# Attention output in four 64x64 quarters, with the state read where it is computed, and a new order of the steps

## Chip, cores and metric

The kernel runs on one core of one Trainium2 chip. The metric is the device time of one run in microseconds. 635.68 us is the median of three runs of the kernel before (635.10 to 636.07).

## What is computed

Three parts follow each other: a linear attention with a decaying state, a mixing layer with sine and cosine, and a gated feed-forward layer. The reference, cut:

```python
# q, k, v, alpha: (4, 8, 768, 48)
for t in range(S):
    state = alpha[:, :, t, :, None] * state + np.einsum('bhd,bhe->bhde', k[:, :, t], v[:, :, t])
    y[:, :, t] = np.einsum('bhd,bhde->bhe', q[:, :, t], state)
...
x = np.ascontiguousarray(attn_out.transpose(0, 2, 1, 3)).reshape(B, S, H * D)   # (4, 768, 384)
theta = x @ w_theta
zr, zi = x * np.cos(theta), x * np.sin(theta)
u = x + np.einsum('ts,bsd->btd', w_tok_r, zr) + np.einsum('ts,bsd->btd', w_tok_i, zi)
x = u + np.maximum(u @ w_ch, 0.0)
...
h = np.maximum(x @ w_in, 0.0)
u, v = h[..., :512], h[..., 512:]
v_n = (v - mean(v)) / sqrt(var(v) + 1e-06)
v_s = np.einsum('ts,bsd->btd', w_spatial, v_n) + b_spatial[None, :, None]
out = (u * v_s) @ w_out
```

## The kernel before

**Units.** The attention is cut into 24 units, `u = 6*b + i`: batch `b` (4) and block `i` of 128 times (6). A unit holds 8 heads, as four pairs `a` of two heads (`par` 0 and 1), and the 128 times as two chunks `c` of 64. On the partitions the heads of a pair stand at 0 to 47 and 64 to 111, or the chunk times of both heads at 0 to 63 and 64 to 127.

**Steps of a unit.** `load_al`, `load_qk`, `load_vn`, `load_vt` are DMAs on SP's queue. VectorE scans the decays (`att_scan`, two scans and a reciprocal) and makes decayed keys and queries (`att_kh`, `att_qh`). TensorE multiplies them: A (`att_a`) gives the 64x64 products of times, which VectorE masks into the tile `am` (`att_mask`, one instruction for each half `e` of the pairs, pairs with `a % 2 == e`); K (`att_k`) transposes the keys, which ScalarE copies out (`att_kt`); U (`att_u`) gives each chunk's addition to the state. VectorE carries the state on from chunk to chunk (`att_s` decays it into the tile `ss`, `att_t` adds U's result). Y (`att_y`) is the output: masked product times values, plus queries times state. ScalarE copies it out of PSUM as `x` (`att_x`). Then TensorE transposes `x` (P, `tr_p`), VectorE splits it into a high and a low part (`tr_l`), TensorE multiplies with `w_theta` (theta, `th_p`, in two halves of 6 and 3 matmuls), ScalarE and VectorE make the sines (`th_k` to `z_m`), the result is split again (`z_h` on ScalarE, `z_l` on VectorE), and TensorE mixes times (T, `tokmix`, six steps of 6 matmuls per unit into the accumulators `acc`). After the six units of a batch come `evac` and the channel layer (`ch_h` to `ch_d`). The last part (`v_p`, `g_u`, `g_s`, `o_p` and what belongs to them) begins near 375 us and isn't touched.

**How Y works before.** Y multiplies both heads of a pair at once, with 96 columns: 112 or 128 partitions go in, and 64 come out for each chunk, so that two chunks stand side by side in the 128x64 form. For this the state and the values must stand block-diagonally: the tiles `sd` and `vd` hold one head's rows against its own 48 columns and zeros elsewhere. `fill` sets the zeros once, on GpSimd; `load_vt` writes the values in two DMAs per unit; `move_s` moves the state out of `ss` in two DMAs per chunk. The output of all heads stands in one PSUM bank. A and U use four 64x64 quarters of the array.

**PSUM.** Five banks are the accumulators of T. Three buffers `ps` are shared by A (two at a time), U (two), K, Y, P, theta and the channel products (one each).

**Weights.** The weights come as float64, are turned into float32 and split by VectorE and ScalarE (`bits`, `join`, `mul`, `low`, `sgn`, `sign`, `mag`, `high`), 30 pieces of them during the first batch. Their DMAs (`raw`) stand on GpSimd's queue.

**Order.** Nothing in a loop sets the order. Each step is entered in a table with its engine, its cost, its buffers and what it waits for. `latest` counts back from due times, to which offsets by the step's name (`OFF`, `OFF0` for the first batch, `OFF3` for the last), unit (`UNIT`) and weight piece (`PIECE`) are added. `order` plays the table through and takes on each free engine the ready step with the earliest time whose buffers are free. The steps are then written out in that order, and each engine works through its own list strictly in it. SP's queue is such a list too.

Of the kernel before, what the change touches and what calls it, by code (L numbers as in the profile page):

```python
# [49 lines left out]
    "bits": 29.93, "sgn": -32.28, "mag": -28.48, "mul": -75.34, "high": -103.47, "low": 39.61, "v": 4.81, "vr": 68.54,  # L50
    "vb": 201.01, "vw": 0.03, "vm": -10.46, "vh": -39.63, "vl": -128.02, "g_u": 6.32, "g_r": -35.97, "g_s": -34.57,
    "g_m": -185.78, "g_h": -102.29, "g_l": 52.98, "o_p": -1.97, "o_e": 72.74, "x2h": 240.17, "x2l": 9.57,
    "x2": -58.05,
# [15 lines left out]
}  # L69
OFF3 = {  # L70
# [21 lines left out]
SSB = 2  # L92
PE_WINDOW = 4096 / 1200
PE_BUSY = {"att_a": 0.78, "att_u": 0.85, "att_y": 0.7}


def order(steps):
# [21 lines left out]
    free = dict.fromkeys(ready, 0.0)  # L119
    port = 0.0  # L120
# [14 lines left out]
    while heap:  # L135
# [11 lines left out]
        while moved:  # L147
            moved = False
            for e, q in ready.items():
# [3 lines left out]
                while q:  # L153
                    _, k = heapq.heappop(q)
# [75 lines left out]
def attention_mixer_kernel(  # L230
# [50 lines left out]
    sdt = []  # L281
    vdt = []
# [871 lines left out]
```

## Time and profile before

| | |
|---|---|
| median of three runs | 635.68 us |
| span of the profiled execution, first to last instruction | 630.0 us |
| median run less span | 5.68 us |
| TensorE matmuls busy | 589.7 us, 94% of the span |
| VectorE busy | 438.3 us, 70% |
| ScalarE busy | 285.1 us, 45% |
| GpSimd busy | 33.0 us, 5% |
| mean DMA rate | 98 GB/s |

The profile is of one execution, of which the page gives the span alone; its whole time is taken as the median, 5.68 us above the span. "Busy" is the union of an engine's instruction times; matmuls overlap in the array, so the time a step costs TensorE is read as the distance from its first matmul to the first one of the next step. Each float32 matmul of the program leaves two records in the trace, so Y's 16 matmuls per part are 32 records together. A row of the timeline gives start, time, engine, source line, operation, written tile and read tiles, and in brackets the idle time ahead of it with what ended it.

### The profile page before, as it was taken

What the parts mean: (1) busy time and instruction counts of PE and PEld (TensorE: products, weight loads), DVE (VectorE), ACT (ScalarE), POOL (GpSimd) and SP (SyncE); (2) the same over time, 40 slices, a digit from 0 to 9 for tenths busy, and PEclk for the clock granted to TensorE, in tenths of its full rate; (3) what the DMA queues carried; (4) which work ended last, traced back from release to release, by engine and by line L of the source; (5) the groups of instructions that cost most, each with busy time, mean ns of one, the idle gap of its engine ahead of it and who ended that gap; (6) DMA issues with size and microseconds to landing.
All of it is one profiled execution on the core that took longest, in us unless ns stands there. A gap on an engine that the chain in (4) does not pass through costs nothing.

```text
span 630.0 us, 13096 instructions
## 1 busy us (share of the span) xinstructions
PE 589.7 (94%) x5364; PEld 545.4 (87%) x5364; DVE 438.3 (70%) x849; ACT 285.1 (45%) x544; POOL 33.0 (5%) x62
## 2 busy tenths in 40 slices
PE   1569789999999999999999999999999999999997
PEld 1458667778888888988889899999999999999997
DVE  7899999999767978676998496866334553454330
ACT  3567677884433345332587444633213431233112
POOL 3111111110000000000000011000000110010000
PEclk9979899999999999999999999999999999999999
DMA  8775555653324432232444545120100100011002
GB/s 234 194 200 165 156 151 164 183 156 101 98 84 125 115 109 75 80 100 84 117 130 129 164 151 201 52 76 25 51 1 1 50 26 1 1 36 41 1 1 75
DMA packets 39228, 61.47 MB, mean 98 GB/s; under 512 B 4864, under 2 KB 30720, under 8 KB 38656
## 3 DMA queue, kind: packets, MB, share of 16 engines
q1 hardware_dynamic: 36768, 48.84, 26.0%
q0 software_dynamic: 2400, 11.80, 6.5%
q8 instruction: 42, 0.69, 0.5%
q14 instruction: 18, 0.15, 0.1%
HBM read 47.94 MB, written 9.44 MB: 91 GB/s over the span
## 4 chain that ended last, share of the span: by engine, by line
PE 80%; DVE 8%; DMA 6%; ACT 3%; issue 1%; SPq 1%; POOL 1%; DVEq 0%; ACTq 0%; POOLq 0%
PE acc L671 20%; PE sp L852 16%; PE psv L795 8%; PE pu L837 8%; PE po L881 8%; PE psc L708 6%; PE psy L568 5%; PE th L610 3%; DMA raw<-in_w_theta 2%; DMA sd<-ss 2%; PE th L613 2%; PE psa L496 1%; PE psu L531 1%; PE psk L514 1%; DVE rt L463 1%
## 5 line engine op out<-in xcount | busy, mean ns | idle before, releaser
L671 PE MATMUL acc<-w,zs 128*128 128x512 f32 (+1 forms) x864 | 175.7, 346 | 0.8 <-ACT w L362 0.8
L671 PEld LDWEIGHTS acc<-w,zs 128*128 128x128 f32 x864 | 134.1, 189 | 19.2 <-ACT w L362 1.0
L852 PE MATMUL sp<-w,vns 128*128 128x384 f32 x576 | 105.1, 336 | 0.0
L852 PEld LDWEIGHTS sp<-w,vns 128*128 128x128 f32 x576 | 100.1, 188 | 0.0
L837 PE MATMUL pu<-xs,w 128*128 128x384 f32 x288 | 55.7, 337 | 0.0
L795 PE MATMUL psv<-w,xs 128*128 128x256 f32 x432 | 55.5, 283 | 0.0
L795 PEld LDWEIGHTS psv<-w,xs 128*128 128x128 f32 x432 | 54.7, 191 | 0.1
L861 DVE TENSOR_TENSOR t<-sp,bsb 128x384 f32<-128x384 f32 x32 | 17.8, 556 | 51.7 <-PE sp L852 51.4
L868 ACT CAST gs<-t 128x384 fp32r<-128x384 f32 x32 | 16.4, 513 | 82.2 <-DVE t L862 77.5
L881 PE MATMUL po<-w,gs 128*128 128x384 f32 x288 | 53.2, 336 | 0.4 <-ACT v L803 0.4
L837 PEld LDWEIGHTS pu<-xs,w 128*128 128x128 f32 x288 | 50.8, 188 | 0.0
L881 PEld LDWEIGHTS po<-w,gs 128*128 128x128 f32 x288 | 49.6, 188 | 0.7 <-ACT v L803 0.7
L568 PE MATMUL psy<-sd,qh 112*64 112x96 f32 x352 | 37.4, 264 | 11.2 <-DVE wf L336 4.0
L708 PE MATMUL psc<-us,wch 128*128 128x256 f32 x324 | 42.2, 284 | 0.0
L708 PEld LDWEIGHTS psc<-us,wch 128*128 128x128 f32 x324 | 40.4, 191 | 0.5
L568 PEld LDWEIGHTS psy<-sd,qh 112*64 112x64 f32 x352 | 25.2, 145 | 17.1 <-issue 8.9
L568 PE MATMUL psy<-vd,am 128*64 128x96 f32 x384 | 37.1, 263 | 0.0
L610 PE MATMUL th<-wth,xh 128*128 128x384 f32 x144 | 31.1, 352 | 6.2 <-DVE xh L600 2.7
L815 POOL TENSOR_TENSOR rs<-rs,mhalf 128x1 f32<-128x1 f32 x24 | 13.7, 571 | 418.7 <-DVE rs L812 418.7
L610 PEld LDWEIGHTS th<-wth,xh 128*128 128x128 f32 x144 | 25.2, 193 | 8.9 <-DVE xh L600 3.5
L496 PE MATMUL psa<-qh,kh 48*64 48x64 f32 x768 | 18.4, 232 | 14.8 <-DVE qh L482 12.8
L496 PEld LDWEIGHTS psa<-qh,kh 48*64 48x64 f32 x768 | 14.6, 141 | 20.3 <-DVE qh L482 12.8
(83 smaller groups left out, 933.9 us busy)
## 6 DMA issues: line engine op xcount, KB each, us to landing
qk<-in_qka SPq DMA_DIRECT2D x24, 448.0 KB, 4.4
al<-in_qka SPq DMA_DIRECT2D x24, 234.5 KB, 3.4
vd<-in_vt SPq DMA_DIRECT2D x48, 96.0 KB, 2.9
raw<-in_w_tr POOLq DMA_DIRECT2D x12, 384.0 KB, 4.3
raw<-in_w_ti POOLq DMA_DIRECT2D x12, 384.0 KB, 3.7
x2d<-xT SPq DMA_DIRECT2D x12, 384.0 KB, 3.1
x<-x2d SPq DMA_DIRECT2D x4, 1152.0 KB, 5.2
out<-o SPq DMA_DIRECT2D x24, 192.0 KB, 1.9
```

The costliest lines, as they stand in the source:

```text
L496: nc.tensor.matmul(st[u]["psa", e][o0:o0 + 64, h, c, :], kh[r0:r0 + D, a, c, :], qh[r0:r0 + D, a, c, :], start=True, stop=True,)
L568: nc.tensor.matmul(psy[64 * c:64 * c + 64, a, :], w, v[:, :, a, :], start=part == 0 or first, stop=part == 1,)
L610: nc.tensor.matmul(th, xh[:, 0, k], wth[:, pr, k], start=(k == 0 and pr == 0), stop=False)
L671: nc.tensor.matmul(acc[b, n][:, c0:c1], zs[:, pl, ri, m * 128:(m + 1) * 128], w[:, pr, t0:t1], start=first and n != 1, stop=last, skip_gro ...
L708: nc.tensor.matmul(ps, wch[:, pl, k, m * 128:(m + 1) * 128], us[:, pr, k], start=(n == 0), stop=(n == 3 * KD - 1),)
L795: nc.tensor.matmul(ps[:, c], xs2[:, pl, k, o:o + 128], w[:, pr, k], start=(n == 0), stop=(n == 3 * KD - 1),)
L815: nc.gpsimd.tensor_tensor(out=s2["rs", b, s], in0=s2["rs", b, s], in1=mhalf, op=ALU.pow)
L837: nc.tensor.matmul(pu, win[f // 2][:, pl, (f % 2) * KD + k], xq[b, h][:, pr, k], start=(n == 0), stop=(n == 3 * KD - 1),)
L852: nc.tensor.matmul(sp[:, :TH], vns[b, s][:, pl, f * 128:(f + 1) * 128], wsp[s][:, pr, h], start=(n == 0), stop=(n == 3 * NS - 1),)
L861: nc.vector.tensor_tensor(out=t1, in0=s2.pop(("sp", b, f, h))[:, :TH], in1=bsb[0][:, t], op=ALU.add)
L868: nc.scalar.copy(out=gs[b][:, 0, f, t], in_=s2["t1", b, f, h])
L881: nc.tensor.matmul(po, gs[b][:, pl, f, s * 128:(s + 1) * 128], wo[f // 2][:, pr, f % 2], start=(n == 0), stop=(n == 3 * KF - 1),)
```

## The change

Y works in quarters. Each head of a pair has its own matmul, 64 stationary columns by 48 moving ones, with the head's own 48 (state) or 64 (values) partitions; the heads of a pair write two PSUM banks, the chunks the two partition halves. The state is read out of `ss` itself (of which there are now six buffers), so `sd`, `move_s` and the fills go, and `vd` is a plain tile, one DMA per unit. The masked product of the pairs with `e == 0` stands at the other head's partitions, so `move_a` moves it (`ax` to `ay`) in two DMAs per unit. `att_x` copies two banks. In the planner, entering and leaving quarters costs time, ready steps of the present form are preferred by 10 us (`TOGETHER`), costs are set anew, and all offsets are new numbers.

```diff
-    "al": 17.11, "qk": 51.36, "vn": -20.22, "vt": -110.25, "sc": 79.43, "kh": 2.45, "q": 22.82, "A": -6.93,
+    "al": -327.26, "qk": -201.91, "vn": 22.23, "vt": -299.27, "sc": 171.11, "kh": 158.5, "q": 48.63, "A": -40.35,
...
-SSB = 2
+SSB = 6
-PE_BUSY = {"att_a": 0.78, "att_u": 0.85, "att_y": 0.7}
+PE_BUSY = {"att_a": 0.85, "att_u": 0.75, "att_y": 0.75}
+QUARTERS = ("att_a", "att_u", "att_y")
+TO_QUARTERS = 0.09
+TO_WHOLE = 0.12
+TOGETHER = 10.0
...
-                    _, k = heapq.heappop(q)
+                    if e == "pe" and TOGETHER:
+                        best = min(q, key=lambda x: (x[0][0] - TOGETHER * (quarters[x[1]] == tiled), x[0][1]))
+                        q.remove(best)
+                        heapq.heapify(q)
+                        k = best[1]
+                    else:
+                        _, k = heapq.heappop(q)
...
+                        if quarters[k] != tiled:
+                            cost += TO_WHOLE if tiled else TO_QUARTERS
+                            tiled = quarters[k]
...
-    def fill(j):
-        nc.gpsimd.memset((vdt, sdt)[j // NB][j % NB], 0.0)
...
     def load_vt(u):
-        vd = vdt[u % NB]
-        for par in range(2):
-            o0 = 64 * (1 - par)
-            nc.sync.dma_start(
-                vd[o0:o0 + 64, :, par].rearrange("p c a e -> p c (a e)"),
-                vt_in[u, par].rearrange("p (c f) -> p c f", c=2),
-            )
+        st[u]["vd"] = pa.tile([128, 2, NP, D], F32, tag="vd", name="vd", bufs=NB)
+        nc.sync.dma_start(st[u]["vd"].rearrange("p c a e -> p (c a e)"), vt_in[u])
...
     def att_mask(u, e):
-        if e == 0:
-            st[u]["am"] = pa.tile([128, 2, 2, 2, 64], F32, tag="am", name="am", bufs=AMB)
+        name = "am" if e else "ax"
+        st[u]["am", e] = pa.tile([128, 2, 2, 64], F32, tag=name, name=name, bufs=AMB)
...
+    def move_a(u):
+        ax = st[u]["am", 0]
+        ay = st[u]["am", 0] = pa.tile([128, 2, 2, 64], F32, tag="ay", name="ay", bufs=AMB)
+        for par in range(2):
+            nc.sync.dma_start(ay[64 * par:64 * par + 64], ax[64 * (1 - par):64 * (1 - par) + 64])
...
-    def move_s(u, c):
-        for par in range(2):
-            r0 = 64 * par
-            nc.sync.dma_start(sdt[u % NB][r0:r0 + D, c, par], st[u]["ss", c][r0:r0 + D])
...
     def att_y(u):
-        qh, am, sd, vd = st[u]["qh"], st[u]["am"], sdt[u % NB], vdt[u % NB]
-        psy = st[u]["psy"] = ps_tile([128, NP, 2 * D], "psy")
+        qh, vd = st[u]["qh"], st[u]["vd"]
+        psy = st[u]["psy"] = [ps_tile([128, NP, D], "psy") for _ in range(2)]
...
-                    if part:
-                        w, v = am[:, a % 2, a // 2, c, :], (vd[:, c, ::-1] if a % 2 else vd[:, c])
-                    else:
-                        w, v = qh[:, a, c, :], sd[:, c]
-                    nc.tensor.matmul(
-                        psy[64 * c:64 * c + 64, a, :], w, v[:, :, a, :],
-                        start=part == 0 or first, stop=part == 1,
-                    )
+                    for par in range(2):
+                        r0 = 64 * par
+                        if part:
+                            w, v = st[u]["am", a % 2][r0:r0 + 64, a // 2, c, :], vd[r0:r0 + 64, c, a, :]
+                        else:
+                            w, v = qh[r0:r0 + D, a, c, :], st[u]["ss", c][r0:r0 + D, a, :]
+                        nc.tensor.matmul(
+                            psy[par][64 * c:64 * c + 64, a, :], w, v,
+                            start=part == 0 or first, stop=part == 1,
+                        )
...
     def att_x(u):
         x = st[u]["x"] = pb.tile([128, DM], F32, tag="x", name="x", bufs=2)
-        nc.scalar.copy(out=x, in_=st[u]["psy"].rearrange("p a e -> p (a e)"))
+        for par in range(2):
+            nc.scalar.copy(out=x.rearrange("p (a w e) -> p a w e", a=NP, w=2)[:, :, par, :], in_=st[u]["psy"][par])
...
-        ka = at("A", "pe", 0.75, att_a, after=[kkh, kqh], tiles=[kh, qh, ps("a", 0), ps("a", 1)])
+        ka = at("A", "pe", 0.51, att_a, after=[kkh, kqh], tiles=[kh, qh, ps("a", 0), ps("a", 1)])
+        kma = at("ms0", "dma", 1.1, move_a, after=km[:1], tiles=[ax, ay])
-        ku = at("U", "pe", 0.7, att_u, after=[kkt, kvn, kvt],
+        ku = at("U", "pe", 0.475, att_u, after=[kkt, kvn, kvt],
...
-        ky = at("Y", "pe", 1.55, att_y, after=[kqh, *km, kvt, *kms], tiles=[qh, am, sd, vd, ps("y")])
-        kx = at("x", "act", 0.375, att_x, after=[ky], tiles=[ps("y"), x])
+        ky = at("Y", "pe", 0.95 if i else 0.71, att_y, after=[kqh, km[1], kma, kvt, *kss],
+                tiles=[qh, am, ay, vd, *hold, ps("y", 0), ps("y", 1)])
+        kx = at("x", "act", 0.62, att_x, after=[ky], tiles=[ps("y", 0), ps("y", 1), x])
```

The host lays `vt` out plainly and gives `vn` the other chunk's values, and U picks its values by `c == par`; its number of matmuls stays. The new lines are one to ten lower in the file: Y is L568 before and L572 now, `z_l` L648 and L653.

**TensorE, one Y.** The program's matmuls of Y of unit 9 before, with the T ahead and behind; `sd_98` and `vd_99` are block-diagonal tiles:

```order
L671 MATMUL acc_557<-w,zs 128x512
L568 MATMUL psy<-sd_98,qh 64x96 x2
L568 MATMUL psy<-vd_99,am 64x96 x2
L568 MATMUL psy<-sd_98,qh 64x96 x2
L568 MATMUL psy<-vd_99,am 64x96 x2
L568 MATMUL psy<-sd_98,qh 64x96 x2
L568 MATMUL psy<-vd_99,am 64x96 x2
L568 MATMUL psy<-sd_98,qh 64x96 x2
L568 MATMUL psy<-vd_99,am 64x96 x2
L671 MATMUL acc_543<-w,zs 128x512
```

The same unit's Y now:

```order
L572 MATMUL psy<-ss,qh 64x48 x4
L572 MATMUL psy<-vd,ay 64x48 x4
L572 MATMUL psy<-ss,qh 64x48 x4
L572 MATMUL psy<-vd,am 64x48 x4
L572 MATMUL psy<-ss,qh 64x48 x4
L572 MATMUL psy<-vd,ay 64x48 x4
L572 MATMUL psy<-ss,qh 64x48 x4
L572 MATMUL psy<-vd,am 64x48 x4
L676 MATMUL acc_1948<-w,zs 128x512
```

Four matmuls of 48 columns stand where two of 96 did, half of the masked ones read `ay`, and a T follows as before.

**TensorE, at the transpose of unit 8.** Before, the last T of unit 5 that fits, the transpose P (`pst`), both halves of theta of unit 8 (`th`) and A (`psa`) of unit 9:

```order
L671 MATMUL acc_681<-w,zs 128x512
L671 MATMUL acc_105<-w,zs 128x256
L587 MATMUL pst<-cst_sb,x 128x128 x3
L610 MATMUL th<-wth,xh 128x384 x6
L613 MATMUL th<-wth,xh 128x384 x3
L496 MATMUL psa<-qh,kh 64x64 x16
L671 MATMUL acc_681<-w,zs 128x512
```

Now, with the T of unit 6 (`acc_101`, `acc_587`) behind A, and theta of unit 8 later:

```order
L676 MATMUL acc_557<-w,zs 128x512
L676 MATMUL acc_558<-w,zs 128x256
L592 MATMUL pst<-cst_sb,x 128x128 x3
L498 MATMUL psa<-qh,kh 64x64 x16
L676 MATMUL acc_101<-w,zs 128x256
L676 MATMUL acc_587<-w,zs 128x512
```

Theta no longer follows its transpose directly; four T of unit 6 and K of unit 10 stand between them. Ahead of theta of unit 8 stand 103 steps of TensorE instead of 96, seven of the difference T.

**VectorE, at the last split of unit 8.** Before, the product `z`, a weight piece, the split of the channel layer (`us`), `zs` of unit 8, and the scan of unit 10:

```order
L600 TENSOR_TENSOR xh<-pst,xh 128x384
L639 TENSOR_TENSOR z<-z,x 128x768
L371 TENSOR_TENSOR wch<-wf,wch 128x384
L696 TENSOR_TENSOR us<-xT,us 128x768
L648 TENSOR_TENSOR zs<-z,zs 128x768
L463 SCALAR_TENSOR_TENSOR rt<-al,heads 112x536
```

Now:

```order
L644 TENSOR_TENSOR z<-z,x 128x768
L547 TENSOR_TENSOR ss<-tmp,rt 112x192
L381 TENSOR_TENSOR w<-wf,w 128x384
L465 SCALAR_TENSOR_TENSOR rt<-al,heads 112x536
L468 RECIPROCAL al<-rt 112x8
L469 SCALAR_TENSOR_TENSOR al<-al,heads 112x536
L653 TENSOR_TENSOR zs<-z,zs 128x768
L605 TENSOR_TENSOR xh<-pst,xh 128x384
```

The scan of unit 11 has moved ahead of this split, and that of unit 10 too, further up. Ahead of it stand 255 steps of VectorE instead of 248.

## Rows read from the trace of the kernel before

**Rows 1.** Busy time of each engine by stage (us), clock, DMA share and rate.

```profile
12.00:46.00 34.00, 20.81 (x283) 17.48 (x284) 30.25 (x63) 20.28 (x41) 4.44 (x8) 0.91 0.74 202
...
95.00:132.00 37.00, 34.85 (x427) 28.62 (x425) 36.45 (x79) 29.39 (x61) 5.37 (x10) 1.00 0.64 182
132.00:375.00 243.00, 242.32 (x2598) 214.53 (x2599) 195.18 (x355) 114.63 (x214) 1.09 (x2) 1.00 0.37 110
```

**Rows 2.** Timeline of TensorE, theta of unit 8: start us, us, instruction.

```profile
132.42 1.33 PE L610 MATMUL th<-wth,xh 128*128 128x384 f32 x6 [0.97 <-ACT xh L591]
133.59 0.76 PE L613 MATMUL th<-wth,xh 128*128 128x384 f32 x3
```

**Rows 3.** TensorE's waits from 133 us: total us, times, longest.

```profile
PE po L881 <- ACT v L803: 0.4, 1, 0.4
```

**Rows 4.** Timeline of TensorE, an A, a T and a Y.

```profile
224.86 0.69 PE L496 MATMUL psa<-qh,kh 48*64 48x64 f32 x32
225.48 1.32 PE L671 MATMUL acc<-w,zs 128*128 128x512 f32 x6
226.73 0.39 PE L568 MATMUL psy<-sd,qh 112*64 112x96 f32 x4
...
228.22 0.39 PE L671 MATMUL acc<-w,zs 128*128 128x256 f32 x1
```

**Rows 5.** Timeline of TensorE, first and late records of a U, and what follows.

```profile
235.71 0.25 PE L531 MATMUL psu<-vn,kt 64*64 64x48 f32 x1
...
236.04 0.22 PE L531 MATMUL psu<-vd,kt 64*64 64x48 f32 x1
...
236.10 0.22 PE L531 MATMUL psu<-vn,kt 64*64 64x48 f32 x1
...
236.31 0.44 PE L613 MATMUL th<-wth,xh 128*128 128x384 f32 x1
```

**Rows 6.** Y's masked products from 132.4 to 375 us: busy us, mean ns.

```profile
L568 PE MATMUL psy<-vd,am 128*64 128x96 f32 x240 | 20.5, 247 | 0.0
```

**Rows 7.** Timeline of VectorE around the last split of unit 8.

```profile
144.51 0.95 DVE L648 TENSOR_TENSOR zs<-z,zs 128x768 fp32r<-128x768 f32 x1
145.38 1.27 DVE L463 TENSOR_TENSOR_SCAN rt<-al,heads 112x536 f32<-112x536 f32 x1
...
148.12 0.33 DVE L336 TENSOR_SCALAR wf<-raw 128x384 uint32<-128x384 uint32 x1
148.37 0.35 DVE L540 TENSOR_TENSOR ss<-tmp,rt 112x192 f32<-112x192 f32 x1
148.64 0.68 DVE L475 TENSOR_TENSOR kh<-qk,rt 112x512 f32<-112x512 f32 x1
149.24 0.54 DVE L621 SCALAR_TENSOR_TENSOR r<-kk,th 128x384 f32<-128x384 f32 x1
149.71 0.68 DVE L482 TENSOR_TENSOR qh<-qk,al 112x512 f32<-112x512 f32 x1
```

**Rows 8.** Timeline of TensorE, theta and the first T of unit 8, a later T.

```profile
147.62 0.68 PE L613 MATMUL th<-wth,xh 128*128 128x384 f32 x3
148.14 1.22 PE L671 MATMUL acc<-w,zs 128*128 128x256 f32 x6
...
163.76 1.32 PE L671 MATMUL acc<-w,zs 128*128 128x256 f32 x6
164.92 1.23 PE L610 MATMUL th<-wth,xh 128*128 128x384 f32 x6
```

**Rows 9.** ScalarE: a cast and a copy of Y (timeline), K's copies (groups).

```profile
225.44 0.84 ACT L643 CAST zs<-z 128x768 fp32r<-128x768 f32 x1 [2.57 <-DVE z L639]
228.33 0.48 ACT L575 COPY x<-psy 128x384 f32<-128x384 f32 x1 [2.05 <-PE psy L568]
...
L518 ACT COPY kt<-psk 128x448 f32<-128x448 f32 x24 | 12.6, 527 | 3.4 <-PE psk L514 3.3
```

**Rows 10.** DMA issues: count, KB each, median us to landing.

```profile
sd<-ss SPq DMA_DIRECT2D x88, 36.0 KB, 2.8
```

More of the change, by code (lines that the diff above doesn't have):

```diff
@@ L43 @@
 OFF = {
[6 rows of a table removed]
[L50 to L53, printed above, removed]
[6 rows of a table added]
+    "bits": 77.01, "sgn": -79.41, "mag": -219.63, "mul": -69.81, "high": -512.86, "low": 41.09, "v": 15.47,
+    "vr": -104.18, "vb": 160.91, "vw": -26.71, "vm": -77.4, "vh": 17.06, "vl": -253.21, "g_u": -6.49, "g_r": -505.32,
+    "g_s": -133.66, "g_m": -268.15, "g_h": -239.6, "g_l": 179.91, "o_p": 16.51, "o_e": -40.8, "x2h": 274.25,
+    "x2l": -16.98, "x2": 30.82,
 }
@@ L63 @@
 OFF0 = {
[5 rows of a table removed]
[5 rows of a table added]
 }
 OFF3 = {
[5 rows of a table removed]
[5 rows of a table added]
 }
 UNIT = {
-    "0": -8.58, "1": -20.17, "2": 19.84, "3": -1.65, "4": -6.97, "5": -16.24, "6": 5.68, "7": -2.87, "8": -8.46,
+    "0": -67.2, "1": -63.66, "2": 30.21, "3": 33.55, "4": 47.8, "5": -60.99, "6": 26.6, "7": 18.11, "8": 16.54,
 }
 PIECE = {
[4 rows of a table removed]
[4 rows of a table added]
 }
@@ L119, in order @@
     free = dict.fromkeys(ready, 0.0)
+    quarters = {k: k[0] in QUARTERS for k in keys}
+    tiled = False
     port = 0.0
@@ L280, in attention_mixer_kernel @@
     NB = 2
-    sdt = []
-    vdt = []
     heads = pa.tile([112, 8, SEG], F32, name="heads")
@@ L285, in attention_mixer_kernel @@
     nc.vector.memset(heads[:, :, 0:1], 1.0)
-    for j in range(NB):
-        sdt.append(pa.tile([112, 2, 2, NP, D], F32, name=f"sd{j}"))
-        vdt.append(pa.tile([128, 2, 2, NP, D], F32, name=f"vd{j}"))
     steps = {}
@@ L501, in att_mask @@
     def att_mask(u, e):
-        if e == 0:
-            st[u]["am"] = pa.tile([128, 2, 2, 2, 64], F32, tag="am", name="am", bufs=AMB)
+        name = "am" if e else "ax"
+        st[u]["am", e] = pa.tile([128, 2, 2, 64], F32, tag=name, name=name, bufs=AMB)
         nc.vector.tensor_tensor(
-            out=st[u]["am"][:, e].rearrange("p h c t -> p (h c) t"),
+            out=st[u]["am", e].rearrange("p h c t -> p (h c) t"),
             in0=st[u]["psa", e].rearrange("p h c t -> p (h c) t"),
@@ L520, in att_u @@
     def att_u(u):
-        vn, kt = st[u]["vn"], st[u]["kt"]
+        vn, vd, kt = st[u]["vn"], st[u]["vd"], st[u]["kt"]
         cs = (0,) if u % NS == NS - 1 else (0, 1)
@@ L528, in att_u @@
                     m = 64 if par == 0 else D
-                    w = par ^ a & 1
-                    v = vn if c == w else vdt[u % NB][:, c, w]
+                    v = vd[:, c] if c == par else vn
                     nc.tensor.matmul(
@@ L910, in mix_time @@
         return START + PACE[0] * min(u, NS) + PACE[1] * max(u - NS, 0) + CHT * (u // NS)
-    for j in range(2 * NB):
-        step(0.0, "pool", 0.75, fill, j)
     for u in range(NU):
@@ L917, in attention_mixer_kernel @@
         al, rt, qk, vn = ("al", 3, u), ("rt", 2, u), ("qk", 2, u), ("vn", 2, u)
-        vd, sd, kh, kt, qh, am = ("vd", 2, u), ("sd", 2, u), ("kh", 1, u), ("kt", 1, u), ("qh", QHB, u), ("am", AMB, u)
+        vd, kh, kt, qh = ("vd", NB, u), ("kh", 1, u), ("kt", 1, u), ("qh", QHB, u)
+        ax, am, ay = ("ax", AMB, u), ("am", AMB, u), ("ay", AMB, u)
         x, xh, kk, r, z, zs = ("x", 2, u), ("xh", 1, u), ("kk", 2, u), ("r", 1, u), ("z", 1, u), ("zs", 3, u)
@@ L935, in attention_mixer_kernel @@
         kvn = at("vn", "dma", 0.5, load_vn, tiles=[vn])
-        kvt = at("vt", "dma", 1.2, load_vt, after=[prev("load_vt"), ("fill", u) if u < NB else None], tiles=[vd])
+        kvt = at("vt", "dma", 0.9, load_vt, after=[prev("load_vt")], tiles=[vd])
         ksc = at("sc", "dve*", 2.7, att_scan, after=[kal, prev("att_scan")], tiles=[al, rt])
@@ L939, in attention_mixer_kernel @@
         kqh = at("q", "dve*", 0.6, att_qh, after=[ksc, kqk], tiles=[qk, al, qh])
-        ka = at("A", "pe", 0.75, att_a, after=[kkh, kqh], tiles=[kh, qh, ps("a", 0), ps("a", 1)])
-        km = [at("m", "dve", 0.33, att_mask, e, after=[ka, ("load_cst",)], tiles=[ps("a", e), am]) for e in range(2)]
+        ka = at("A", "pe", 0.51, att_a, after=[kkh, kqh], tiles=[kh, qh, ps("a", 0), ps("a", 1)])
+        km = [
+            at("m", "dve", 0.33, att_mask, e, after=[ka, ("load_cst",)], tiles=[ps("a", e), am if e else ax])
+            for e in range(2)
+        ]
+        kma = at("ms0", "dma", 1.1, move_a, after=km[:1], tiles=[ax, ay])
         k = at("K", "pe", 0.4, att_k, after=[kkh, ("load_cst",)], tiles=[kh, ps("k")])
         kkt = at("kt", "act", 0.42, att_kt, after=[k], tiles=[ps("k"), kt])
-        ku = at("U", "pe", 0.7, att_u, after=[kkt, kvn, kvt],
+        ku = at("U", "pe", 0.475, att_u, after=[kkt, kvn, kvt],
                 tiles=[kt, vn, vd] + [ps("u", c) for c in range(1 if final else 2)])
-        kms = []
+        kss = []
         ktx = ("att_t", u - 1, 1) if i else None
@@ L953, in attention_mixer_kernel @@
                 k = at(f"s{c}", "dve*", 0.27, att_s, c, after=[ksc, ktx], tiles=[rt, *ss, *tmps_in])
-                kms.append(at(f"ms{c}", "dma", 0.9, move_s, c, after=[k, prev("att_y", back=2), ("fill", NB + u) if u < NB else None], tiles=[*ss, sd]))
+                kss.append(k)
             if not (final and c):
                 ktx = at(f"t{c}", "dve", 0.27, att_t, c, after=[k, ku], tiles=[ps("u", c), ("tmp", 1, (u, c)), *ss])
-        ky = at("Y", "pe", 1.55, att_y, after=[kqh, *km, kvt, *kms], tiles=[qh, am, sd, vd, ps("y")])
-        kx = at("x", "act", 0.375, att_x, after=[ky], tiles=[ps("y"), x])
+        hold = [("ss", SSB, (u, c)) for c in range(2) if i or c]
+        ky = at("Y", "pe", 0.95 if i else 0.71, att_y, after=[kqh, km[1], kma, kvt, *kss],
+                tiles=[qh, am, ay, vd, *hold, ps("y", 0), ps("y", 1)])
+        kx = at("x", "act", 0.62, att_x, after=[ky], tiles=[ps("y", 0), ps("y", 1), x])
         kp = at("P", "pe", 0.3, tr_p, after=[kx, prev("th_p", 1)], tiles=[x, ps("t")])
@@ L1120, in _layout @@
     v = f["v"].reshape(B, NP, 2, NS, 2, 64, D).transpose(0, 3, 2, 5, 4, 1, 6)
-    sw = v.copy()
-    sw[..., 1::2, :] = v[:, :, ::-1][..., 1::2, :]
-    vt = sw.reshape(NU, 2, 64, DM)
-    vn = np.stack([sw[:, :, c, :, c] for c in range(2)], axis=2).reshape(NU, 128, NP * D)
+    vt = v.reshape(NU, 128, DM)
+    vn = np.stack([v[:, :, 1 - c, :, c] for c in range(2)], axis=2).reshape(NU, 128, NP * D)
     cst = np.zeros((128, 192), q.dtype)
```

38 rows, old and new, of tables (OFF, OFF0, OFF3, PIECE) are left out of this document.

## The prediction

> **What bounds the kernel now.** I read the windows by stage first. Until 132 us VectorE is the limit: it is busy 36.45 of 37 us in the last stage before that and 30.25 of 34 in the first long one, while TensorE has idle time [rows 1]. From 132 us it is the other way round: TensorE is busy 242.32 of 243 us, VectorE 195.18. The timeline shows the last stop of weight: TensorE waits 0.97 us before the first theta matmuls of unit 8 at 132.42 us, for the copy that follows a transpose [rows 2]. Behind it the list of TensorE's waits is headed by 0.4 us, a single one [rows 3]. So from there the end of the span is TensorE's queue added up, 630.0 - 132.4 = 497.6 us, at the granted clock 1.00 [rows 1]. A microsecond taken from TensorE behind that point shortens the run by a microsecond, as long as VectorE delivers in time. Ahead of it, it only adds to TensorE's idle time.
>
> **Y itself (`att_y`).** In the steady stretch Y starts at 226.73 and the next step at 228.22: 1.49 us [rows 4]. It is 16 rounds of two matmuls side by side. The new Y is 16 rounds of four, each with 64 stationary and 48 moving columns. No row shows Y in that form; the nearest is A, which loads 64 stationary columns into four quarters, 32 records in 8 rounds, and holds TensorE from 224.86 to 225.48, 0.62 us [rows 4]. Y needs eight rounds more. U, also four quarters and 48 moving columns, starts its last 64x64 records 0.06 us apart [rows 5]. So Y becomes 0.62 + 8 x 0.06 = 1.10 us, and saves 0.39. Bounds: if the moving columns set the pace, two times U, which takes 0.60 (235.71 to 236.31), less one entry and exit: about 1.0, saving 0.5. If the four quarters did not overlap better than two, 16 rounds at today's pace: nothing saved. I take 0.39, since A has the same 64 stationary columns. The steps into and out of quarters cost TensorE something (the 0.62 of A holds it), but Y already pays such a change today, and the new order hardly puts A, U and Y side by side: counted through both orders, 134 changes of array shape before and 131 now (Y's 128x64 counted as a shape of its own). I price that at nothing.
>
> The Trainium skill ("TensorE: Matmul & The Clock Gate", Part 3, What overlaps and what doesn't) says that a weight load overlaps running matmuls only where the row group differs. In the new Y two of four quarters share each row group, so by that rule a round would cost two loads one after the other. A shows the opposite: its 32 loads and matmuls, two quarters to a row group, pass in 0.62 us. By the rule Y would take 2.1 us and the kernel 643 (worked out with the rivals), by the row 1.10 and 629.7; I go by the row.
>
> **How many Ys count.** From 132.4 us on, 240 of the records that multiply the masked product stand in the trace, 16 to a unit: 15 units, 9 to 23 [rows 6]. The other nine lie in VectorE's stage and give nothing.
>
> **The new order.** It moves where VectorE holds TensorE. Unit 8 shows it. Its last split (`z_l`, L648) ends when the next instruction starts, 145.4 us, and frees its token-mix matmuls T, which TensorE reaches at 148.14 [rows 7, 8]. Counted down VectorE's new order, ahead of that split stand two scans, one `att_kh`, one `att_qh`, one `att_s`, and one each of `mul`, `low`, `join`, `bits` more, one `sgn` and one `tr_l` fewer. By starts in the timeline: a scan step 145.38 to 148.12, 2.74; `att_kh` 0.60 (`att_qh`, the same shape, as much); `att_s` 0.27; a 128x384 operation on two inputs 0.47, as L621 from 149.24 to 149.71; `bits` and `sgn` 0.25 each and cancel [rows 7]. That is 5.48 + 1.20 + 0.27 + 2 x 0.47 = 7.9 us, so the split ends at 153.3, if VectorE stays as full as it is now.
>
> In exchange TensorE has more behind it by then: six T, one A and one K more, two theta halves fewer. T is 1.16 us (163.76 to 164.92), the halves are 1.17 and 0.52 [rows 2, 8]; K lies between nothing and A's 0.62, and I take 0.3. Left for TensorE from the first T of unit 8: now 630.0 - 148.14 = 481.9; then 481.9 - 6 x 1.16 - 0.62 - 0.3 + 1.69 = 475.7, less 14 Ys (10 to 23) at 0.39 = 5.5: 470.2. The end comes to 153.3 + 470.2 = 623.5 us. Unit 8's theta, the binding place today, has seven T (8.1 us) more ahead of it in the new order and four steps more on VectorE: it no longer binds. TensorE's idle time moves from there to the T's of units 7 to 9.
>
> **What is added at small price.** The copy out of PSUM (`att_x`) becomes two of 192 columns. Today 384 columns start at 228.33 and take 0.48, 448 take 0.53, so about 0.08 per 100 columns and 0.32 for one of 192 (an estimate from these two): ScalarE is done 0.65 us after Y's end instead of 0.48 [rows 9]. One T, 1.16 us, stands between Y and its transpose P in most late units and covers it with 0.5 us to spare. Without that cover each P would wait. I book 0.5 us for all of them, between 0 and 0.5 a unit.
>
> `move_a` adds two DMAs of 64 KB a unit between the mask and Y. They replace four moves of 36 KB, whose median from issue to landing is 2.8 us [rows 10]. In the new order the shortest way from A to Y in units 9 to 23 is U, K and T's of some 5 us of TensorE work (unit 20); the mask and a landing of 2.8 us fit into it. The queue behind a waiting `move_a` on SP holds the loads of later units; the old state moves stood there in the same way, four where there are two now. At unit 7, in VectorE's stage, Y will wait for its move, and that wait is covered by VectorE's lead over unit 8. If not, it costs up to 2.8 us. VectorE's instructions are the same in number and form.
>
> The four fills on GpSimd go, behind which the second piece of `w_theta` is asked for today. Against that stands `cst_sb`, which moves behind a load that waits for `att_qh` of unit 0. VectorE has 3.75 us free between 12 and 46 us [rows 1], so that is the most that the start can give; I take nothing.
>
> **Sum:** 623.5 + 0.5 = 624.0 us of span, 6.0 less than 630.0. The median of the runs shown, 635.68, lies 5.68 above that span; I carry this unchanged: 629.7.
>
> **The rivals.**
> - *The start and VectorE's first stage get shorter too* (fills gone, state moves gone, Y no longer waiting for state): 3.75 us more, down to about 626 in time. For: these waits are there. Against: VectorE is busy 30.25 of those 34 us already, and new waits come for old.
> - *VectorE's stage gets longer*: `move_a` (2.8 us) or late loads stop it once or twice, and the split of unit 8 ends 3 to 4.5 us later: 632.6 to 634.1.
> - *Two PSUM banks of three* (the slower side). Y now takes two of the three buffers that A, U, K, P and theta share, and holds them until the second copy. Where ScalarE is in a `z_h` cast (0.84 us [rows 9]) when Y ends, the copies end 0.84 + 0.65 = 1.5 us after Y, 0.3 us past one T; P waits, and A or U cannot start either. At 0.45 us a unit over 14 units the gain is gone; at 0.9 the time is 630.0 - 6.6 + 12.6 + 5.7 = 642. Against: ScalarE is idle half of that stretch, 2.05 us ahead of the copy shown. The Trainium skill ("TensorEngine Tiling (Array Packing)", PSUM Bottleneck and Gotcha 1) warns of just this, that emptying PSUM is not sped up by tiling; no row shows it here yet.
> - *The row groups serialize*: two loads to a round, 16 x 2 x 0.06 + 0.15 = 2.1 us for Y, 0.6 more than now, over 14 units 8.4: 630.0 - 1.1 + 8.4 + 5.7 = 643. A's 0.62 us speaks against it.
> - *Nothing*: VectorE limits longer than I count and takes back what Y gives: 634.4 to 637.
>
> **How the numbers follow.** Chances: forecast (626.5 to 632) 0.60; shorter start 0.12; longer first stage 0.14; no change 0.05; two banks 0.07; row groups 0.02. 0.2% of 635.68 is 1.3 us, about what a measurement can tell. Faster: 0.60 + 0.12 + 0.14 = 0.86; same 0.05; slower 0.09. The range must leave out no more than 2 in 10: 624.0 to 634.0, from the shorter start to the longer first stage.
>
> **What the changed profile would show.** Y: four records per round, 1.05 to 1.15 us to the next step, at clock 1.00. TensorE's last wait of weight at T of unit 7, 8 or 9, near 143 to 168 us, for VectorE's split; nearly none behind it. ScalarE's two copies near 0.32 us each. Wrong would be: waits of TensorE for ScalarE's copy at P, A or U in each unit (two banks); Y at 1.5 us or more (quarters don't overlap); VectorE waiting for loads, or Y for `ay`, before 130 us by more than now.

## The result, and the profile after

The changed kernel took 624.39 us (median of four runs, 623.99 to 625.89), the kernel before 635.39 beside it: ratio 0.984 (0.981 to 0.986), 11.0 us. Measured again later it took 625.05 (five runs) against 634.27: 0.986 (0.984 to 0.988). The forecast was 629.7: right in sign and 5 us too high. The time lies inside the stated range (624.0 to 634.0), by 0.4 us, and below the 626.5 to 632 that the forecast gave as its own.

Windows by stage after the change (columns as in [rows 1]):

```profile
12.00:46.00 34.00, 23.20 (x343) 19.23 (x344) 32.88 (x68) 21.84 (x46) 3.76 (x7) 1.00 0.70 196
95.00:132.00 37.00, 32.71 (x465) 27.11 (x464) 35.85 (x76) 26.57 (x55) 4.29 (x8) 0.95 0.63 180
132.00:375.00 243.00, 242.16 (x3140) 215.48 (x3139) 198.39 (x369) 117.40 (x234) 2.70 (x4) 1.00 0.38 112
```

The picture is that of before [rows 1]: VectorE full until 132 us, TensorE from there. TensorE's waits from 134 us to the end (answering to [rows 3]) are a single one:

```profile
PE acc L676 <- DVE acc L685: 0.8, 1, 0.8
```

The timeline of TensorE after: the last wait, the T's around unit 8's split, and a whole Y between two T's (answering to [rows 2, 4, 8]).

```profile
134.70 1.55 PE L676 MATMUL acc<-w,zs 128*128 128x256 f32 x7 [0.75 <-DVE acc L685]
...
151.85 2.36 PE L676 MATMUL acc<-w,zs 128*128 128x512 f32 x12
...
223.70 1.28 PE L676 MATMUL acc<-w,zs 128*128 128x512 f32 x6
224.91 0.33 PE L572 MATMUL psy<-ss,qh 48*64 48x48 f32 x8
225.06 0.30 PE L572 MATMUL psy<-vd,ay 64*64 64x48 f32 x8
...
225.76 0.30 PE L572 MATMUL psy<-vd,am 64*64 64x48 f32 x8
225.99 0.50 PE L676 MATMUL acc<-w,zs 128*128 128x512 f32 x1
```

Y starts at 224.91 and the next T at 225.99: 1.08 us for 64 records (eight rows of eight, three of them shown), where 32 took 1.49 [rows 4]; Y before has eight matmuls in each of its two parts, 16 in all. Of the twelve T records at 151.85 the second six are the first T of unit 8, so it starts at about 153.0. VectorE at that place, and ScalarE's copies of a Y, a little further on (answering to [rows 7, 9]):

```profile
151.61 0.93 DVE L653 TENSOR_TENSOR zs<-z,zs 128x768 fp32r<-128x768 f32 x1
152.46 0.55 DVE L605 TENSOR_TENSOR xh<-pst,xh 128x384 fp32r<-128x384 f32 x1
...
226.10 0.54 ACT L580 COPY x<-psy 128x192 f32<-128x192 f32 x2 [1.23 <-PE psy L572]
```

Unit 8's last split ends at 152.5. ScalarE waits 1.23 us for Y and has both copies done at 226.64, 0.65 us after Y's end. The DMA issues (columns as in [rows 10]) list the new move:

```profile
ay<-ax SPq DMA_DIRECT2D x48, 64.0 KB, 3.1
```

Where the time went is best read by cutting each span at TensorE's last wait of weight near 135 us: ahead of the cut VectorE decides, behind it TensorE's queue. Of the kernel before there are two profiles, of the changed one also two. The rows of the cut of the other profiles follow with the experiments.

| kernel | span | after the last wait at | from there to the end | Y |
|---|---|---|---|---|
| before, first profile | 630.0 | 132.42 | 497.6 | 1.49 |
| before, second profile | 633.2 | 135.83 | 497.4 | 1.48 |
| changed, first | 622.2 | 134.70 | 487.5 | 1.08 |
| changed, second | 622.5 | 135.06 | 487.4 | 1.08 |
| changed, Y of the old length | 630.3 | 136.64 | 493.7 | 1.52 |
| changed, extra products early | 625.9 | 138.61 | 487.3 | 1.08 late |
| changed, extra products late | 632.6 | 136.90 | 495.7 | 1.65 late |

So the gain lies behind the cut: 10.0 us. Fifteen Ys at 0.40 are 6.0 of them; the other 4.0 are mostly steps that TensorE now does ahead of the cut (summed to the next step, T takes 121.7 us behind it where it took 125.1). The cut itself moves little for that: it comes 0.8 to 1.1 us earlier than in the second profile of before and 2.3 to 2.6 later than in the first.

### The profile page after: what moved, and what is told of

It reads as the page before. It is cut to its first block, busy times and chain, and to the rows that moved or that the text cites. A ratio compares the mean times of both kernels' runs of the same rounds, so it can differ in the third digit from the quotient of the medians.

```text
span 622.2 us, 14431 instructions
## 1 busy us (share of the span) xinstructions
PE 586.0 (94%) x6100; PEld 542.2 (87%) x6100; DVE 435.2 (70%) x849; ACT 287.2 (46%) x568; POOL 30.5 (5%) x58
## 4 chain that ended last, share of the span: by engine, by line
PE 84%; DVE 9%; DMA 4%; ACT 2%; issue 1%; DVEq 0%; ACTq 0%; POOLq 0%
PE acc L676 22%; PE sp L857 16%; PE psv L800 8%; PE pu L842 8%; PE po L886 8%; PE psc L713 6%; PE th L615 4%; PE psy L572 4%; PE psa L498 2%; PE th L618 2%; PE psu L538 2%; DMA raw<-in_w_ti 1%; DVE rt L465 1%; DVE wf L353 1%; PE psk L522 1%; PE pst L592 1%
## 5 line engine op out<-in xcount | busy, mean ns | idle before, releaser
L676 PE MATMUL acc<-w,zs 128*128 128x512 f32 (+1 forms) x864 | 178.9, 351 | 0.8 <-DVE acc L685 0.8
L676 PEld LDWEIGHTS acc<-w,zs 128*128 128x128 f32 x864 | 136.8, 193 | 18.9 <-DVE acc L685 1.2
L713 PE MATMUL psc<-us,wch 128*128 128x256 f32 x324 | 42.7, 284 | 0.0
L877 DVE TENSOR_TENSOR gs<-t,gs 128x384 fp32r<-128x384 f32 x32 | 17.5, 555 | 35.9 <-ACT gs L873 35.6
L713 PEld LDWEIGHTS psc<-us,wch 128*128 128x128 f32 x324 | 40.6, 190 | 0.6
L850 ACT ACTIVATE ur<-pu 128x384 f32<-128x384 f32 x32 | 15.7, 491 | 48.8 <-DVE t L867 36.6
L372 ACT CAST w<-wf 128x384 fp32r<-128x384 f32 x48 | 24.3, 509 | 17.7 <-DMA wf<-in_w_sp 11.5
L498 PE MATMUL psa<-qh,kh 48*64 48x64 f32 x768 | 20.0, 237 | 12.8 <-DVE qh L484 11.8
L498 PEld LDWEIGHTS psa<-qh,kh 48*64 48x64 f32 x768 | 15.9, 144 | 18.3 <-DVE qh L484 11.8
```

What stands on the lines that cost most here:

```text
L372: nc.scalar.copy(out=c["part"](0), in_=f)
L498: nc.tensor.matmul(st[u]["psa", e][o0:o0 + 64, h, c, :], kh[r0:r0 + D, a, c, :], qh[r0:r0 + D, a, c, :], start=True, stop=True,)
L676: nc.tensor.matmul(acc[b, n][:, c0:c1], zs[:, pl, ri, m * 128:(m + 1) * 128], w[:, pr, t0:t1], start=first and n != 1, stop=last, skip_gro ...
L713: nc.tensor.matmul(ps, wch[:, pl, k, m * 128:(m + 1) * 128], us[:, pr, k], start=(n == 0), stop=(n == 3 * KD - 1),)
L877: nc.vector.tensor_tensor(out=gs[b][:, 1, f, t], in0=s2.pop(("t1", b, f, h)), in1=gs[b][:, 0, f, t].bitcast(F32), op=ALU.subtract)
```

## The experiments

**The kernel before, again.** No edit.

> The kernel before, unchanged, for the spans and clocks of more of its runs. Theory (TensorE's queue sets the end, about 1.8 us lie around any span, as in the changed kernel's 623.99 against 622.2): its timed runs span 632.5 to 634.5, longer than the one profiled span of 630.0, and the difference stands ahead of 132 us, where VectorE limits. Rival (what lies around the span is 5.7 us in the kernel before and shrinks with the change): spans of 629.5 to 630.5 at totals of 635 to 636.

635.03 us, ratio 1.000 (0.998 to 1.002). The profiled execution has a span of 633.2 us in 635.02, so 1.8 us lie around the span, not 5.68; the twelve runs span 630.5 to 635.5. The theory holds. The timeline of TensorE shows the same last wait as [rows 2], 3.4 us later, and VectorE's `z_l` of unit 8 ends at 148.8 instead of 145.4:

```profile
135.83 1.31 PE L610 MATMUL th<-wth,xh 128*128 128x384 f32 x6 [0.92 <-ACT xh L591]
...
147.93 0.95 DVE L648 TENSOR_TENSOR zs<-z,zs 128x768 fp32r<-128x768 f32 x1
148.80 1.27 DVE L463 TENSOR_TENSOR_SCAN rt<-al,heads 112x536 f32<-112x536 f32 x1
```

The profile on which the prediction rested was a short execution of this kernel: its 630.0 us lie below all of the 77 other spans on record (630.2 to 638.2, median 632.6). It is 3.2 us shorter than this profile, all of it won before the cut.

**The old Y in the new order.** The steps of the kernel before, written out in the order of the changed one; each move of the state stands right after its `att_s`, as soon as Y of two units before is past; the fills stand first, `ss` has three buffers instead of two.

```diff
-SSB = 2
+SSB = 3
...
-        for key in order(latest(steps, due)):
+        for name in SEQUENCE:
+            key = by_name[name]
             runs[key](*key[1:])
```

> The old Y (96 columns, block-diagonal tiles, state moved by DMA, one bank) with the steps written out in the order of the changed kernel. Theory (behind 132 us each Y counts with its 0.40 us, the early ones don't): 15 x 0.40 = 6.0 us above the changed kernel, about 630.4. Rival, the order alone brings the gain: 624 to 625. Rival, all 24 Ys count: 634.

683.36 us, ratio 1.075 (1.072 to 1.078): outside all three. TensorE's waits over the whole span (total us, times, longest) say why:

```profile
PE psy L743 <- DMA sd<-ss: 39.4, 16, 5.3
PE psa L671 <- DVE qh L657: 13.7, 1, 13.7
```

In the new order Y stands close behind `att_s`, as only a state read in place allows. With the moves put back, Y waits 39.4 us for them; in the first profile of before those waits are 2.1 us. The run answers nothing about the order alone, but shows that this order, with the moves put where they are here, needs the state in place.

**Extra products, late and early.** In the changed kernel the state products of Y are issued twice in units 9 to 23, or in units 0 to 8. The second write replaces the first, so only time is added.

```diff
+                        if part == 0 and u >= 9:
+                            nc.tensor.matmul(psy[par][64 * c:64 * c + 64, a, :], w, v, start=True, stop=True)
                         nc.tensor.matmul(
```

(early: `u < 9`)

> Changed kernel, with the products of queries and state issued twice in units 9 to 23 (the first ones are overwritten): 8 rounds of 0.058 us more in 13 units, half of the matmuls in two. Theory: 13 x 0.47 + 2 x 0.23 = 6.5 us more, about 631. Rival (there is slack in TensorE's queue behind 132 us, or the gain came from elsewhere): under 2 us more.

633.97 us, ratio 0.999 (0.998 to 1.000).

> The same doubling in units 0 to 8, ahead of the point where TensorE's queue takes over. Theory: hidden behind VectorE, 0 to 1 us more, 624.4 to 625.4. Rival, all Ys count: 7 x 0.47 + 2 x 0.23 = 3.7 us more, 628.

627.9 us, ratio 0.990 (0.987 to 0.992). The rows of the cut, late and early, one timeline of TensorE each:

```profile
136.90 1.32 PE L678 MATMUL acc<-w,zs 128*128 128x256 f32 x6 [0.76 <-DVE acc L687]
```

```profile
138.61 1.55 PE L678 MATMUL acc<-w,zs 128*128 128x256 f32 x7 [0.18 <-DVE acc L687]
```

A Y with the extra products takes 1.65 us, 0.57 more, where 0.47 was expected. Fifteen of them make 8.4 (13 at 0.57 and two with half of the products at 0.50); behind the cut there are 8.3 more, and the time is 8.9 above the changed kernel measured again: late Ys count one for one. The early ones add about 5 us of TensorE work and 2.9 us of time. Behind the cut nothing changes (487.3); the cut comes 3.6 us later than in the second profile of the changed kernel. But 2.0 of these stand at the end of the first stage already: the first `z_l` starts at 44.74 instead of 42.77, and it does so too (44.96) in the run with late products, whose early units are unedited. So between 1.6 and 2.9 us come from the early Ys, against the prediction, which gave them nothing.

**The changed kernel again, Ys of the old length in every unit, and the fills put back.** The second doubles the state products of three of the four pairs, so that Y takes 1.52 us in all 24 units; the third puts four fills back on GpSimd, into a tile that nothing reads.

```diff
+                        if part == 0 and a < 3:
+                            nc.tensor.matmul(psy[par][64 * c:64 * c + 64, a, :], w, v, start=True, stop=True)
```

```diff
+    for j in range(4):
+        step(0.0, "pool", 0.75, fill, j)
```

> The changed kernel unchanged, beside the four below and the same runs of the kernel before, because its first time (624.39 us) came from another call than the two kernels with doubled products (633.97 and 627.9 us). If the chip and the hour make no difference, 624.4 us again (623.9 to 626), ratio 0.984, and the early doubling is worth the whole 3.5 us. If the two profiles with doubled products began late (their first score scan ended at 10.3 and 8.4 us where the changed kernel's profile shows 8.6, their first z_l at 45.7 and 45.9 where it shows 43.1), the changed kernel comes at 626 to 627 us here, and the early doubling is worth 1.5 us or less.

625.05 us, ratio 0.986 (0.984 to 0.988): inside the first band, 0.7 us above the first time, so 0.7 of the early 3.5 us lie between the two measurements of the changed kernel.

> The part-0 products of three of the four head pairs are issued twice in every unit, first copy overwritten, so the output step Y takes about 1.08 + 0.43 = 1.51 us in all 24 units, as long as in the kernel before (1.48 us); order, banks, state in place and everything else stay as changed. Theory that the length of Y is the whole of the gain, in early units too: 15 late Ys by 0.43 is 6.5 us, nine early ones by 0.43 by the share 3.5/5.1 seen with the early doubling is 2.7 us, so 633.6 us (632.5 to 635), level with the kernel before. Theory that only the Ys behind the last wait count and the new order gives the rest: 624.4 + 6.5 = 630.9 us. If state in place and the missing tiles were what matters: under 628 us.

633.05 us, ratio to the kernel before 0.998 (0.996 to 1.000), 8.0 us over the changed kernel. The theory that Y's length is nearly all of the gain holds. The timelines at the cut, of the changed kernel again and of the one with old lengths:

```profile
135.06 1.32 PE L676 MATMUL acc<-w,zs 128*128 128x256 f32 x6 [0.75 <-DVE acc L685]
```

```profile
136.64 1.55 PE L678 MATMUL acc<-w,zs 128*128 128x256 f32 x7 [0.32 <-DVE acc L687]
```

The cut moves by 1.6 us, of 9 x 0.43 = 3.9 us put in ahead of it; these two profiles start alike (first `z_l` at 42.77 and 42.76). Behind the cut 493.7 - 487.4 = 6.3 us are added, 15 x 0.42. With Ys as long as before, everything else in the change (the new order, the state in place, two banks, the missing tiles) is worth 1.2 us by the medians (0.2 to 2.3 by the interval).

VectorE's waits up to the end of unit 8's `z_l` show a part of how early Ys come to count. With old lengths they hold

```profile
DVE xh L607 <- ACT xT L603: 0.9, 2, 0.5
DVE xh L607 <- ACT xh L598: 0.3, 1, 0.3
```

where the changed kernel has 0.4 us in all. This is the split of `x` (`tr_l`), which stands behind Y, its copy and its transpose. It makes 0.8 us of the 1.4 by which VectorE is idle longer there; the rest was not traced to a Y.

> The changed kernel with the four fills of the block-diagonal tiles put back on GpSimd at the start (into a tile that nothing reads). Theory: GpSimd is idle in its first microseconds beside casts that nobody waits for, so 624.4 us, within 0.3% of the changed kernel. Rival (shorter start): the fills hold up the first units, and their removal was worth up to 3 us: 627 us.

624.81 us, 0.2 below the changed kernel beside it: GpSimd's time in the fills is worth nothing. That no step has to wait for a filled tile any more isn't tested by this, since nothing reads the tile here.

**The plan with other prices and other tables.** Four kernels with the new Y.

```diff
-TO_QUARTERS = 0.09
-TO_WHOLE = 0.12
-TOGETHER = 10.0
+TO_QUARTERS = 0.0
+TO_WHOLE = 0.0
+TOGETHER = 0.0
```

> The changed kernel planned with both mode-switch prices and the price of steps that pull together set to zero: the same tables, but 336 of 460 TensorE steps stand at another place, with the same 131 changes between quarter steps and whole steps. Theory that the order matters only through what TensorE waits for in the first 135 us: 625 to 628 us, its Ys as short as in the changed kernel. Rival that counting the switches is what makes the order good: 630 us or more, with Ys or A steps that take longer than 1.08 and 0.62 us, or with waits of TensorE behind 135 us.

654.05 us, ratio 1.032 (1.029 to 1.034): the rival. Y still takes 1.08 us in the median. TensorE's waits from 137 us are new:

```profile
PE psc L713 <- ACT us L697: 3.2, 1, 3.2
PE psy L572 <- DVE xT L722: 2.7, 1, 2.7
```

The second kernel keeps `TOGETHER = 10.0` and sets only the two prices to zero; the third has 0.08 and 0.13 for them.

> The changed kernel planned with the two prices of a mode switch at zero, but with the pull of 10.0 for steps of one mode kept, since planning without all three came out at 654 us: TensorE idle 48.2 us in its trace instead of 32.3, with waits as late as 385 us. Theory that the planner's clock has to know the switches, or its order drifts against the chip: 640 us or more, with TensorE waits behind 300 us again. Rival that the pull was what the order lost: 624 to 632 us.

646.58 us, ratio 1.019 (1.016 to 1.022): as the theory said; the control that follows shows that this time alone does not prove it.

> A control for the run without switch prices: the prices stay, at 0.08 and 0.13 instead of 0.09 and 0.12, which is no better or worse a description of the chip; the order stays the same for its first 470 rows on TensorE and then changes in over 2000 lines. Theory that counting the switches is what makes the order good: 624 to 628 us. Rival that the tables of due-time corrections fit one order only, so that any other number in the planner breaks it, whatever it stands for: 640 us or more, with TensorE waits behind 135 us.

633.61 us, ratio 0.999 (0.997 to 1.000), between the two expectations: the whole gain is gone, for a change of prices by 0.01 us. Its waits of TensorE from 137 us:

```profile
PE psc L713 <- ACT us L697: 2.1, 1, 2.1
PE psy L572 <- DVE xT L722: 1.6, 1, 1.6
PE psc L713 <- DVE us L701: 1.1, 1, 1.1
```

Its last wait near 135 us ends at 134.6, as in the changed kernel, and Y takes 1.08. Windows at the places of those waits show what is lost:

```profile
298.00:304.00 6.00, 4.42 (x75) 4.03 (x69) 5.56 (x10) 3.28 (x5) 0.00 (x0) 1.00 0.60 173
304.00:310.00 6.00, 6.00 (x75) 5.14 (x65) 6.00 (x15) 3.83 (x9) 0.00 (x0) 0.72 0.68 211
365.00:376.00 11.00, 7.35 (x51) 6.34 (x50) 10.49 (x22) 4.29 (x8) 1.13 (x1) 1.00 0.13 36
```

TensorE is idle 1.6 and 3.7 us at the channel layer of a batch (L713 is its product). In the first stretch a Y waits until VectorE has taken the channel products out of PSUM (L722), in the second the products wait for their operands (L697, L701). Behind the first of these waits the granted clock is 0.72 over 6 us (part of it at 1.2 GHz, the rest at 2.4), 1.7 us of work. That is 7.0 of the 8.3 us by which the span is longer.

The fourth has the changed kernel's prices and the tables of offsets of the kernel before.

> The changed kernel with the tables of due-time corrections of the kernel before: quarters, state in place and counted switches alone. Theory that the gain is that of the Ys and the tables are only worth some 2 us: 24 shorter Ys as seen in the changed kernel give 634.3 - 8.0 = 626 us (624 to 629). Rival that tables set for one order break another: 640 us or more, slower than the kernel before although each Y takes 1.08 us.

647.39 us, ratio 1.020 (1.017 to 1.023): the rival. TensorE waits at the channel layer here too:

```profile
PE psc L713 <- ACT us L697: 2.5, 1, 2.5
```

Each of the four other plans that were tried breaks the fit of tables and prices. A hair off costs 8.6 us and zero prices 21.5, but since even the hair breaks the fit, how much of that is the counting itself stays open.

**The new Y in the old order.** The mirror image of the second run: the changed kernel's steps, written out in the order of the kernel before; fills and state moves fall away, `move_a` stands right behind the first mask of its unit.

```diff
-        for key in order(latest(steps, due)):
+        for name in SEQUENCE:
+            key = by_name[name]
             runs[key](*key[1:])
```

> The new output step (quarters, two banks, state read in place, no tiles to fill) run in the order of the kernel before, step by step, written out instead of planned; the state's moves fall away, the one move of part-1 scores that the new step needs stands right behind the first mask of its unit. It separates the step from the order, as the run with Ys of the old length in the new order (633.05 us) did from the other side. Theory that most of the gain is the shorter Y in either order: 15 late Ys by 0.40 is 6.0 us, the nine early ones count for some 0.4 of their 3.6 us, so 634.2 - 7.4 = 626.8 us (625 to 628.5), and the order gives the remaining 1 to 2 us. Rival that the short step is only worth its time in an order planned for it, as the runs with other tables (647 us) and other prices (633.6 us) suggest: 630 to 634 us, with TensorE waits behind 135 us that the kernel before does not have.

666.4 us, ratio 1.050 (1.047 to 1.053): worse than the rival allowed. TensorE's waits from 137 us are headed by

```profile
PE psy L744 <- DMA ay<-ax: 12.7, 20, 2.3
```

and its timeline shows one of them in the middle of a Y:

```profile
241.16 0.33 PE L744 MATMUL psy<-ss,qh 48*64 48x48 f32 x8
242.44 0.31 PE L744 MATMUL psy<-vd,ay 64*64 64x48 f32 x2 [0.95 <-DMA ay<-ax]
243.07 0.27 PE L744 MATMUL psy<-vd,ay 64*64 64x48 f32 x3 [0.31 <-DMA ay<-ax]
```

The first state products run, then Y stands until the moved scores land. In the old order Y follows its mask closely, since there the mask was read in place. Over the whole span Y waits 16.9 us for the move, 22 times; in the changed kernel it is 0.6 us, once. Windows by stage and around that wait:

```profile
132.00:375.00 243.00, 225.06 (x2956) 195.65 (x2957) 178.79 (x326) 106.02 (x215) 1.07 (x2) 0.95 0.33 95
...
242.00:248.00 6.00, 5.25 (x98) 4.34 (x99) 1.47 (x4) 0.54 (x2) 0.00 (x0) 0.72 0.43 123
```

TensorE is idle 17.9 of 243 us where it was idle 0.7 [rows 1], and the granted clock is 0.95 on average.

## Why the prediction was right, and where it failed

**What bounds the kernel:** right. Late work on TensorE counts one for one (8.3 of 8.4 us of extra products behind the cut).

**Y:** right. 1.08 us against 1.10, taken from A's 64 columns and U's 0.06 us. By the Trainium skill ("TensorE: Matmul & The Clock Gate", Part 3, What overlaps and what doesn't), a weight load overlaps running matmuls only where the row group differs. The trace disagrees: the prediction's estimate by that rule was 2.1 us, and 64 loads and 64 matmul records, two quarters to a row group, pass in 1.08.

**Fifteen Ys count, nine give nothing:** the first half is right, the second is the step that failed in the mechanism. Of 3.9 us put into early Ys, 1.6 reach the cut, of about 5 us 1.6 to 2.9. VectorE is nearly full in that stage, 35.85 of 37 us, but the cut moves with TensorE's work all the same, in part at VectorE's waits for the transposed `x`.

**The new order:** the two numbers of the sum hold. Unit 8's split ends at 152.5 (forecast 153.3); from its first T at 153.0 TensorE has 469.2 us left (forecast 470.2). The binding place was wrong: not the T's of units 7 to 9 but the first T of unit 6 at 134.70, which waits 0.75 us for VectorE to empty an accumulator (`evac`, L685). T of unit 8 comes 0.5 us behind its split and doesn't wait. The forecast hit the sum with a place that doesn't bind because its margin is that small; that is luck in part. The 0.8 us between 152.5 and 153.3 are mostly VectorE's extra work ahead of the split, 7.2 us (busy 142.91 against 135.66, shown below) instead of 7.9.

**Small prices:** the two copies end 0.65 us after Y, as estimated, and no P, A or U waits for them behind 134 us, so the 0.5 us booked was not spent. The two-banks rival does not show here: ScalarE is the one that waits, 1.23 us ahead of the copies shown and 28.0 us ahead of all 48. The Trainium skill ("TensorEngine Tiling (Array Packing)", PSUM Bottleneck and Gotcha 1) warns that tiling does not speed up the emptying of PSUM; in this trace that emptying is no limit. `move_a` takes 3.1 us to land instead of 2.8 and is hidden; the old order shows the price without that cover, up to 2.3 us a unit behind 137 us. GpSimd's time in the fills gives nothing, as taken.

**The sum:** the span is 622.2, 1.8 below the forecast 624.0; 0.3 of that is the place of unit 8's T, 1.0 what is left behind it, 0.5 the copies. The largest miss is the last line, the 5.68 us carried unchanged from span to median. Only 1.8 us lie around a span. The other 3.9 were the distance of one short execution from the median, a first stage 3.4 us quicker than in the second profile. Carrying them took for granted that the changed kernel would start as late as the kernel before does as a rule. VectorE's busy time up to the end of unit 8's `z_l` (stretch, length, busy time and instructions, granted clock, DMA share, GB/s) says where they went, for the two profiles of before, the two of the changed kernel and the one with old lengths:

```profile
0.00:145.38 145.38, 135.66 (x279) 0.95 0.63 176
0.00:148.80 148.80, 135.93 (x280) 0.92 0.63 172
0.00:152.46 152.46, 142.91 (x290) 0.98 0.60 173
0.00:152.81 152.81, 142.80 (x290) 0.93 0.61 172
0.00:154.39 154.39, 143.00 (x290) 0.94 0.60 171
```

VectorE's idle time is length less busy time: 9.7 and 12.9 us before, 9.6 and 10.0 in the changed kernel, 11.4 with old lengths. So "as full as it is now" holds against the short execution; against the second profile, nearer to the typical one, VectorE loses 2.9 to 3.3 us of idle time, and the carried lateness is not there. The shorter early Ys account for about 1.4 of that; the cause of the rest stays open. With 1.8 us instead of 5.68 the sum gives 624.0 + 1.8 = 625.8, 0.8 from the second median.

**Rivals:** "shorter start" gave 626, nearest the measured time, and it holds in part: against the second profile VectorE has those 2.9 to 3.3 us less idle time ahead of unit 8's split, against the first, from which the rival was worked out, 0.2 less and 0.3 more. Between 12 and 46 us its idle time fell as the rival says, from 3.75 to 1.12 us in the first profiles; before 12 us it rose from 3.68 to 5.85, with a wait of 4.7 us for a piece of `w_theta`. "Longer first stage", "two banks", "row groups" and "nothing" are refuted.

So the 9.2 us of the later measurement are 8.0 from the shorter Y (6.3 late, 1.7 early, once the order is given), and 1.2 from all the rest. But the order is not free. The old Y in the new order costs 49 us over before, the new Y in the old order 31, each with its moves placed directly behind what they read and no other placing tried; tables or prices that don't fit cost 8.6 to 29 us over the changed kernel.

## What to carry to other kernels

A step with other latencies and the order around it are one change: a faster step lost 31 us here in the order of the slower one, so tune the order with the step, and test the step alone by stretching it to its old length within the new order, which keeps the order and all of its moves. Before a sum is carried from a profile to a median, take the time and the span from the same execution, and look whether that execution is a typical one; if it is not, ask whether the change keeps what makes the others later. A stage in which another engine is busy 97% of the time is not one in which this engine's time is worth nothing: here about two fifths of it still counted (1.6 of 3.9 us).

## What the runs showed of the hardware

- Extra state products written to the same place cost 0.57 us for 32 records, 0.071 for four, about as much as new ones (1.08 us for 64 is 0.068 for four).
- A step into or out of quarters costs TensorE about 0.1 us. Behind 135 us in the changed kernel a T takes 1.05 us in the median between two steps of the whole array, 1.16 behind a step in quarters, 1.15 ahead of one and 1.25 between two.
- A wait of a microsecond or two can cost TensorE more than itself, and need not. In the old order with the new Y it stands idle for 0.95 and 0.31 us just ahead of 243.1 us, and the granted clock is 0.72 over 242 to 248 us (part of that stretch at 1.2 GHz, the rest at 2.4). With prices a hair off, 1.57 us of idle time are followed by 0.72 over 304 to 310 us, but 2.06, 1.10 and 0.49 us between 367 and 375 us by 1.00 over 376 to 388 us. In the old order the granted clock is 0.95 over 132 to 375 us, where the changed kernel has 1.00: up to 12 us of full-clock time on top of the idle time.
- A lower clock in the first 48 us hardly showed while VectorE led: the changed kernel's two profiles have 1.00 and 0.89 as granted clock there and 0.994 and 0.983 over the whole, and spans of 622.2 and 622.5 us.
